# A second place for the next expert's transposed rows in an attention and mixture-of-experts kernel

## The chip, the core and the metric

The kernel runs on one core of one Trainium2 chip. The metric is the device time of one execution in microseconds; the median of three executions of the kernel before is 756.62 us (755.61 to 757.49). The core's engines are called PE (TensorE), ACT (ScalarE), DVE (VectorE), POOL (GpSimd) and SP (SyncE, which here issues most of the DMAs). Each of them works through its own instructions in order, and waits on semaphores for the others.

## What is computed

The reference first does causal attention with a decay, for 8 batches, 8 heads, 576 positions and 64 columns per head, and reshapes the result to 4608 rows of 512 columns. Then it does a mixture of eight experts, each row in one expert:

```
logits = x @ w_gate;  e_idx = argmax(logits, axis=1)
gate_w = softmax(logits) at e_idx;  eom = sigmoid(x @ w_output_gate)
for e in range(8):
    mask = e_idx == e
    h  = maximum(x[mask] @ w1[e], 0)        # 512 -> 1024
    ye = h @ w2[e]                          # 1024 -> 512
    out[mask] = gate_w[mask] * eom[mask, e] * ye
```

The change touches only the second half, from about 345 us on.

## The kernel before

All values are carried as two 16-bit parts (a high part in f16 and the rest), so a product is made of three matmuls. The attention stage also computes for each of its rows the expert, the row's rank in it and its weight; it writes the rows to a DRAM buffer `xbuf`. The instructions of each engine stand in the order in which the program text makes them (`manual_schedule`), so every line of the text sets a place in each queue it touches.

**The experts.** Expert 0 is done first, with rows of early batches and plain products (`up`, `down`). Expert 1 follows. The other six are ordered by how many rows they have: a small chain on DVE (lines 1396 to 1425) sums up the counts, sorts them, and writes `rank` (which expert comes n-th) and `ids` (its rows and weights). The n-th expert is given a fixed capacity, `CAPS` = 640, 608, 592, 576, 560, 512 rows; expert 1 has 640. Rows beyond these capacities go to lists of overflow (`overflow_slots`, lines 1016 to 1052), which the loop at the end of the program works off; it has no work here, but its count `ncum` must be loaded into a register of every engine (line 1485).

**Up products (`up_seven`).** The product with `w1` is done blockwise with seven block products in place of eight: weights and rows are first added and subtracted in blocks. For the weights this is `weights_pair` (four of them per expert): DVE makes sums in PSUM, POOL (or DVE, with `pool=False`) makes the difference `xr` in SBUF, ACT makes the high parts, DVE and POOL the low ones. For the rows it is `rows_whole` (POOL, four additions of high and low part into f32 tiles `x`) and `rows_sums` (called for k = 0 and 1: DVE subtracts, ACT casts, DVE makes the low part, four times). Each `up_seven` runs four rounds `p` of seven products (each product six matmuls); ACT copies three partial results of a round to `keep` (`kept`, line 1289), where DVE takes them up in its additions (lines 1313, 1317, 1323). The last product of a round is put into the next round; that of the last round is made within the first down tile (`finish_up`). Twice per round `between(p, half)` does side work, numbered `fc` = 0 to 7: ACT and POOL split one block of `w2`, SP fetches another, POOL gathers rows of the next expert, SP fetches its `w1`.

**Rows of the next expert.** `gather_rows(x, t)` is an indirect DMA from POOL of 128 rows into `xg[:, t]`; `gather_turn(x, t)` is a DMA transpose from SP's queue of those rows into `xT`. `rows_x` makes the tile `xT` in a pool with one buffer. In the kernel before it is always the pool `m2`:

```
if nx:
    x1 = rows_x(m2, nx["ids"])
```

so the next expert's transposes write where the current expert's products read.

**Down products.** For each tile of 128 rows `down_sum` makes 24 matmuls of 512 columns into one of two PSUM banks `y`; ACT scales it into `ys` (line 1102) and POOL writes it out by indirect DMA (line 1106). The rest of a capacity beyond whole tiles is done by `down_narrow` in parts of 64 and 32 rows, which DVE evicts (lines 1131, 1133); the last tile of the last expert is done in two halves of columns (`down_halves`). Beside tile `t` of the down products stands a piece of work for the next expert: before the change a `weights_pair` beside t = 0, 1, 3 and 4, `rows_whole` at t = 1 ahead of its pair, and both `rows_sums` beside t = 2.

PSUM tiles for sums come from one ring of three banks (`hp1`), which block products, `weights_pair` and `rows_sums` share.

Of the kernel before, what the change touches and what calls it, by code (L numbers as in the profile page):

```python
# [9 lines left out]
F32 = mybir.dt.float32  # L10
# [10 lines left out]
P = 128  # L21
# [3 lines left out]
E = 8  # L25
# [16 lines left out]
CAP = 640  # L42
CT = CAP // P
FIXED = 2
# [5 lines left out]
ET = 3  # L50
# [27 lines left out]
def _attn_moe(ctx, tc, qk, vm, f, wg, w1, w2, out):  # L78
# [937 lines left out]
    def overflow_slots():  # L1016

        with tc.tile_pool(name="ov", bufs=1) as ov:
            g = [ov.tile([P, E, G], F32, name=f"ov{j}") for j in range(3)]
            start, eid = [ov.tile([P, E, G], BF16, name=f"g{j}") for j in range(2)]  # L1020
            me, caps = [ov.tile([P, n], F32, name=f"c{n}") for n in (1, E)]
            for t, pattern, base in ((start, [[0, E], [P, G]], 0), (eid, [[1, E], [0, G]], 0)):
                nc.gpsimd.iota(t, pattern=pattern, base=base, channel_multiplier=0,
                               allow_small_or_imprecise_dtypes=True)
            nc.gpsimd.iota(me, pattern=[[0, 1]], base=1, channel_multiplier=1, allow_small_or_imprecise_dtypes=True)
            for r, cap in enumerate(CAPS + [CAP] * FIXED):
                nc.gpsimd.memset(caps[:, r:r + 1], float(cap))
            mine = ov.tile([P, E, E], F32, name="mine")
            own, over = [ov.tile([P, E], F32, name=n) for n in ("own", "over")]
            nc.vector.tensor_tensor(mine, key.unsqueeze(2).broadcast_to([P, E, E]),  # L1030
                                    top.unsqueeze(1).broadcast_to([P, E, E]), op=ALU.is_equal)
            nc.vector.tensor_tensor(mine, mine, caps.unsqueeze(1).broadcast_to([P, E, E]), op=ALU.mult)
            nc.vector.tensor_reduce(own, mine, axis=AX.X, op=ALU.add)
            nc.vector.tensor_tensor(over, cnt, own, op=ALU.subtract)
            fl = lambda t: t.rearrange("p e g -> p (e g)")
            valid, cum, base = g
            nc.vector.tensor_tensor(valid, over.unsqueeze(2).broadcast_to([P, E, G]), start, op=ALU.is_gt)
            nc.vector.tensor_tensor_scan(fl(cum), fl(valid), fl(valid), 0.0, op0=ALU.add, op1=ALU.max)
            nc.vector.scalar_tensor_tensor(fl(base), fl(eid), float(NT), fl(start), op0=ALU.mult, op1=ALU.add)
            nc.vector.tensor_tensor(base, base, own.unsqueeze(2).broadcast_to([P, E, G]), op=ALU.add)  # L1040

            nc.vector.scalar_tensor_tensor(fl(valid), fl(cum), me, fl(valid), op0=ALU.is_equal, op1=ALU.mult)
            res = ov.tile([P, 2], F32, name="res")
            for j, src in ((1, base), (0, eid)):
                nc.vector.tensor_tensor(base, src, valid, op=ALU.mult)
                nc.vector.tensor_reduce(res[:, j:j + 1], fl(base), axis=AX.X, op=ALU.add)
            resi = ov.tile([P, 2], I32, name="resi")
            nc.vector.tensor_copy(resi, res)
            nc.sync.dma_start(slots, resi)
            ncum = cp.tile([1, 1], I32, name="ncum")  # L1050
            nc.vector.tensor_copy(ncum, fl(cum)[0:1, E * G - 1:E * G])
        return ncum
# [208 lines left out]
    def up_seven(ws, x, sums, cap, h, between):  # L1261
# [21 lines left out]
            nc.vector.scalar_tensor_tensor(hl[:, fc, sl], m, 0.0, hh[:, fc, sl], op0=ALU.max, op1=ALU.subtract)  # L1283
            yield

        keep = ar.tile([P, 2048], F32, name="x")[:, 0:6 * CAP // 2].rearrange("p (j n) -> p j n", j=6)

        def kept(j, m):
            nc.scalar.copy(out=keep[:, j, 0:n], in_=m)  # L1289
# [8 lines left out]
        for p in range(HF):  # L1298
            w = ws[p]
            y = staged(n, "hp0")  # L1300
            product(y, w, A11, rows_of_half(0, 0), True)
            p1 = kept(p % 2, y)
            z = staged(n)
            product(z, w, S1, rows_sum(T1), True)
            p5 = kept(2 + p % 2, z)
            if open_:
                last_product(*open_)
            between(p, 0)
            product(y, w, S2, rows_sum(T2), False)
            u2 = kept(4 + p % 2, y)  # L1310
            v = staged(n)
            product(v, w, A12, rows_of_half(1, 0), True)
            nc.vector.tensor_tensor(v, v, p1, op=ALU.add)  # L1313
            product(z, w, S4, rows_of_half(1, 1), False)
            c11, c12 = split(v, p, 0), split(z, p, 1)
            next(c11)
            nc.vector.tensor_tensor(z, z, u2, op=ALU.add)
            next(c11)
            next(c12)
            between(p, 1)  # L1320
            product(y, w, S3, rows_sum(T3), False)
            u = staged(n, "y")
            nc.vector.tensor_tensor(u, y, p5, op=ALU.add)
            next(c12)
            for _ in split(u, p + HF, 1):
                pass
            open_ = p, w, y
# [5 lines left out]
    with tc.manual_schedule(engines=ENGINES):  # L1333
# [3 lines left out]
        feats_out(NQ - 1)  # L1337
        W1r = {fc: fetch_w1(m2, w1[1], fc, 8) for fc in PAIRS}
        AHEAD = 4
        slot = m1.tile([P, CT], F32, name="slot")  # L1340
        nc.gpsimd.iota(slot, pattern=[[P, CT]], base=0, channel_multiplier=1, allow_small_or_imprecise_dtypes=True)
        beyond = m1.tile([P, len(CAPS), CT], F32, name="beyond")
# [38 lines left out]
            gather_turn(x1, t)  # L1381
        first_splits(1, 2)
        down_out(x, down_sum(W2, h, 0), 0)
        first_splits(2, 3)
        down_out(x, down_sum(W2, h, 1), 1)
        first_splits(3, HF)
        down_out(x, down_sum(W2, h, 2), 2)
        sums = rows_whole(x1, CAP)
        up(W1, x, [(EARLY, CAP)], h)
        for k in range(2):  # L1390
            rows_sums(sums, CAP, k)
        down(W2, xl, h, ET, CT)
        W1, W2, x = W1n, [], x1

        cnt_ps = pr.tile([P, 512], F32, name="ms", bufs=1)
        nc.tensor.matmul(cnt_ps[:, 0:E], ones16, runs, start=True, stop=True)
        cnt = cp.tile([P, E], F32, name="cnt")
        nc.vector.tensor_copy(cnt, cnt_ps[:, 0:E])
        nc.vector.tensor_tensor(cnt[:, 0:1], cnt[:, 0:1], late, op=ALU.add)
        tie, key, top = [m1.tile([P, E], F32, name=n) for n in ("tie", "key", "top")]  # L1400
        rank = m1.tile([P, E], I32, name="rank")
        nc.gpsimd.iota(tie, pattern=[[1, E]], base=0, channel_multiplier=0, allow_small_or_imprecise_dtypes=True)
        nc.gpsimd.memset(tie[:, 0:FIXED], -1e6)
        nc.vector.scalar_tensor_tensor(key, cnt, float(E), tie, op0=ALU.mult, op1=ALU.add)
        nc.vector.max(top, key)
        nc.vector.tensor_copy(rank, top)
# [8 lines left out]
        for j in range(2):  # L1415
            each = m1.tile([P, R, CT, E], F32, name="each")
            shape = [P, R, CT, E]
            nc.vector.tensor_tensor(each, acc[:, j].rearrange("p e t -> p t e").unsqueeze(1).broadcast_to(shape),
                                    mine.unsqueeze(2).broadcast_to(shape), op=ALU.mult)
            if j:  # L1420
                nc.vector.tensor_reduce(ids[:, :, :, 1].bitcast(F32), each, axis=AX.X, op=ALU.add)
            else:
                own = m1.tile([P, R, CT], F32, name="own")
                nc.vector.tensor_reduce(own, each, axis=AX.X, op=ALU.add)
                nc.vector.tensor_tensor(ids[:, :, :, 0], own, beyond, op=ALU.add)

        def expert(r):

# [7 lines left out]
        for n in range(len(CAPS) + 1):  # L1436
# [2 lines left out]
            nx = expert(n) if n < len(CAPS) else None  # L1439
            nt = -(-nx["cap"] // P) if nx else 0  # L1440
            if nx:
                x1 = rows_x(m2, nx["ids"])

            def between(p, half):
                fc = 2 * p + half
                W2.append(split_w2(W2r[fc], nc.gpsimd))
                if fc + AHEAD < NF:
                    W2r.append(fetch_w2(e["w2"], fc + AHEAD))
                if nx:
                    if 2 <= fc < 2 + nt:  # L1450
                        gather_rows(x1, fc - 2)
                    if fc >= NF - AHEAD:
                        g = PAIRS[fc - NF + AHEAD]
                        W1r[g] = fetch_w1(m2, nx["w1"], g, 8)

            finish_up = up_seven(W1, x, sums, cap, h, between)
            W1n, W2n = [], []
            for t in range(nt):
                gather_turn(x1, t)
            for t in range(tiles):  # L1460
                if nx is None and t == tiles - 1:
                    down_halves(W2, x, h, t)
# [3 lines left out]
                if nx:  # L1466
                    for g in PAIRS[2 * t + AHEAD:2 * t + AHEAD + 2]:
                        W1r[g] = fetch_w1(m2, nx["w1"], g, 8)
                    if t == 1:
                        sums_n = rows_whole(x1, nx["cap"])  # L1470
                    if t == 2:
                        for k in range(2):
                            rows_sums(sums_n, nx["cap"], k)
                    else:
                        W1n.append(weights_pair(W1r, len(W1n)))
                    if t == 3:
                        W2r = [fetch_w2(nx["w2"], fc) for fc in range(AHEAD)]
# [1 line left out]
                    down_narrow(W2, x, h, t, rest)  # L1479
                else:  # L1480
                    down_out(x, y, t)
                if n == 0 and t == 3:
                    ncum = overflow_slots()
                if n == 2 and t == 0:
                    nsl = nc.values_load(ncum, min_val=0, max_val=(NT - min(CAPS)) // P + E)
            if nx:
                e, x, W1, W2, sums = nx, x1, W1n, W2n, sums_n
# [73 lines left out]
```

## Time and profile before

| | us |
|---|---|
| median of three executions | 756.62 |
| the profiled execution, its whole time | 753.45 |
| its span, first to last instruction | 751.7 |
| PE matmuls busy | 693.3 (92% of the span) |
| POOL busy | 551.9 (73%) |
| DVE busy | 519.7 (69%) |
| ACT busy | 415.4 (55%) |

A line of the timeline has the start and the length in us, the engine, the line of the program, the operation, the tile written and the tiles read, the shapes, how many instructions are merged, and in brackets how long the engine was idle before it and whose work ended that wait. Matmuls overlap in the array: those of 512 columns show 0.38 us each but start every 0.215 us.

### The profile page before, as it was taken

To read this page: it belongs to the slowest core of one execution; us is meant where nothing else is said; L and a number is where in the kernel's file an instruction comes from. 1 tells how busy PE (TensorE), PEld (TensorE's weight loads), DVE (VectorE), ACT (ScalarE), POOL (GpSimd) and SP (SyncE) were. 2 spreads that over 40 slices of the span, in tenths; PEclk is the share of its full clock that TensorE was granted. 3 is DMA by queue.
4 is the path that set the end of the run, shared out by engine and by line. 5 is a ranking of instruction groups with operands and counts; after the bars stand their busy time and mean duration, and the time that the engine had idled before them with its cause. 6 is when DMAs were issued, how large, how long until landed. Compare 5 with 4: busy or idle time off the path is not lost. (4 is left out here: it accounts for less than half of the span.)

```text
span 751.7 us, 22240 instructions
## 1 busy us (share of the span) xinstructions
PE 693.3 (92%) x8823; PEld 460.1 (61%) x8842; DVE 519.7 (69%) x1175; ACT 415.4 (55%) x990; POOL 551.9 (73%) x618
## 2 busy tenths in 40 slices
PE   4999999999999999989989949989979899799896
PEld 2577777777777777765746426547447366374564
DVE  7576798999989978778575574555585576656640
ACT  4456666667666756654345436456456465464641
POOL 9879799999899989824436745767757687687632
PEclk9999999999999999999999978999999999999999
DMA  4436577667766663394815604824917638348101
GB/s 153 157 120 181 161 186 191 182 168 167 190 174 170 149 172 75 98 228 129 188 63 155 195 28 157 210 90 154 238 48 187 199 101 204 132 154 224 60 15 39
DMA packets 119452, 110.72 MB, mean 147 GB/s; under 512 B 82669, under 2 KB 92077, under 8 KB 119344
## 3 DMA queue, kind: packets, MB, share of 16 engines
q1 hardware_dynamic: 108566, 71.50, 37.8%
q10 hardware_dynamic: 4618, 18.88, 7.7%
q0 software_dynamic: 6160, 18.88, 7.6%
q8 instruction: 70, 1.15, 0.6%
q14 instruction: 38, 0.31, 0.2%
HBM read 72.47 MB, written 19.49 MB: 122 GB/s over the span
## 5 line engine op out<-in xcount | busy, mean ns | idle before, releaser
L434 POOL TENSOR_TENSOR plo<-p 128x512 f16<-128x512 f32 x182 | 194.4, 1087 | 21.5 <-PE mx L305 11.6
L1276 PE MATMUL hp<-xT,sh 128*128 128x320 f16 (+5 forms) x784 | 152.8, 295 | 21.8 <-ACT x L1289 17.0
L432 ACT ACTIVATE p<-sc 128x512 f32<-128x512 f32 x192 | 111.6, 595 | 60.6 <-PE sc L305 58.5
L336 DVE TENSOR_REDUCE nR<-mx 128x2 f32<-128x1024 f32 (+4 forms) x154 | 121.3, 805 | 34.4 <-PE mx L305 32.0
L1276 PE MATMUL hp<-xT,sl 128*128 128x320 f16 (+5 forms) x392 | 115.3, 294 | 0.0
L305 PE MATMUL sc<-qk 64*128 64x64 f32 (+5 forms) x644 | 114.0, 432 | 0.0
L1090 PE MATMUL y<-w2h,hh 128*128 128x512 f16 x272 | 103.7, 381 | 5.2 <-ACT ys L1102 5.2
L1276 PEld LDWEIGHTS <-sh 128*128 128x128 f16 x784 | 77.6, 100 | 50.1 <-issue 24.9
L1092 PE MATMUL y<-w2h,hl 128*128 128x512 f16 x272 | 103.7, 381 | 1.2 <-issue 0.2
L1091 PE MATMUL y<-w2l,hh 128*128 128x512 bf16 x253 | 96.4, 381 | 0.0
L1010 POOL TENSOR_TENSOR w2l<-w2r,w2h 128x512 bf16<-128x512 f32 x56 | 64.7, 1157 | 37.9 <-ACT w2h L1009 31.0
L305 PEld LDWEIGHTS <-pick 64*128 64x128 bf16 (+1 forms) x1152 | 55.0, 97 | 55.1 <-issue 41.7
L1281 ACT ACTIVATE hh<-hp 128x320 f16<-128x320 f32 (+5 forms) x84 | 34.9, 417 | 60.1 <-DVE hp L1313 31.0
L505 PE MATMUL av<-Vs,p 128*128 128x65 f16 x640 | 65.9, 193 | 1.3 <-ACT xr L552 1.3
L506 PE MATMUL av<-Vs,p 128*128 128x64 bf16 x640 | 65.7, 195 | 0.0
L507 PE MATMUL av<-Vs,plo 128*128 128x65 f16 x640 | 65.4, 192 | 0.0
L1106 POOL DMA_INDIRECT out_dram<-ys,idsr x28 | 28.0, 999 | 49.1 <-ACT ys L1102 35.4
L305 PE MATMUL mx<-qk 64*128 64x512 bf16 (+3 forms) x372 | 54.9, 308 | 8.5 <-DMA qk<-in_qk_dram 5.9
L505 PEld LDWEIGHTS <-p 128*128 128x128 bf16 x640 | 59.1, 97 | 5.5 <-issue 5.3
L1283 DVE SCALAR_TENSOR_TENSOR hl<-hp,hh 128x320 f16<-128x320 f32 (+5 forms) x84 | 38.6, 459 | 33.2 <-ACT hh L1281 27.3
L506 PEld LDWEIGHTS <-p 128*128 128x128 bf16 x640 | 59.4, 97 | 1.4 <-issue 1.4
L507 PEld LDWEIGHTS <-plo 128*128 128x128 f16 x640 | 59.4, 99 | 0.0
(262 smaller groups left out, 1826.2 us busy)
## 6 DMA issues: line engine op xcount, KB each, us to landing
qk<-in_qk_dram ACTq DMA_DIRECT2D x31, 576.0 KB
w1r<-in_w_dram SPq DMA_DIRECT2D x64, 256.0 KB
w2r<-in_w_dram SPq DMA_DIRECT2D x64, 256.0 KB
v<-in_vm_dram SPq DMA_DIRECT2D x15, 576.0 KB
xbuf<-x SPq DMA_DIRECT2D x16, 512.0 KB
Eq<-mts SPq DMA_DIRECT2D x64, 0.1 KB
xbuf<-x SPq DMA_DIRECT2D x16, 64.0 KB
xT<-x SPq DMA_TRANSPOSE x62
```

What stands on the lines that cost most here:

```text
L305: nc.tensor.matmul(dst(i), w(i), x(i), start=start, stop=stop)
L336: nc.vector.tensor_reduce(o, x, axis=AX.X, op=ALU.max, negate=True)
L432: nc.scalar.activation(out=f32, in_=src, func=AF.Exp, scale=0.125)
L434: eng.tensor_tensor(lo, f32, upper(f32), op=ALU.subtract)
L505: nc.tensor.matmul(dst, ph, vv[:, 0:W], start=kc == 0, stop=False)
L506: nc.tensor.matmul(dst[:, 0:D], ph, vv[:, W:].bitcast(BF16), start=False, stop=False)
L507: nc.tensor.matmul(dst, pl, vv[:, 0:W], start=False, stop=kc == qc)
L1010: eng.tensor_tensor(l, raw, h, op=ALU.subtract)
L1090: nc.tensor.matmul(y, hh[:, fc, sl], wh, start=j == 0, stop=False)
L1091: nc.tensor.matmul(y, hh[:, fc, sl], wl, start=False, stop=False)
L1092: nc.tensor.matmul(y, hl[:, fc, sl], wh, start=False, stop=j == NF - 1)
L1276: nc.tensor.matmul(m, w[part][:, j, k], b(q, k), start=first and k == i == 0, stop=k == 1 and i == 2, skip_group_check=True)
```

## The change

Six edits, all in the expert stage:

- The next expert's `xT` is taken from `m2` for odd n and from the pool `ar` for even n. `gather_rows` moves from `fc` 2 to 6 to `fc` 0 to 4, and `gather_turn` from behind `up_seven` into `between`, two steps behind its gather.
- `rows_whole` moves from t = 1 to ahead of the first down tile; `rows_sums` is made for k = 0 beside t = 1, ahead of the pair that is there, and for k = 1 beside t = 2.
- `keep` has a tile of its own with three slots, in place of six slots in a tile of `x`.
- The chain of counts, ranks and `ids` moves from behind expert 0 into it, behind the first down tile; its constants `tie` are made earlier.
- The fourth weight pair of expert 1 (`first_splits(3, HF)`) moves from behind down tile 1 of expert 0 to behind the row sums.
- `overflow_slots` moves from t = 3 of expert 1 to t = 0 of the last expert, with three of its tiles in an old tile `x16`, and the load of its count moves from the third expert of the loop to the last one's last tile but one.

```diff
@@ overflow_slots
-            g = [ov.tile([P, E, G], F32, name=f"ov{j}") for j in range(3)]
+            g = ar.tile([P, 1280], F32, name="x16", bufs=2)[:, 0:3 * E * G]
+            g = [g[:, j * E * G:(j + 1) * E * G].rearrange("p (e g) -> p e g", g=G) for j in range(3)]
@@ up_seven
-        keep = ar.tile([P, 2048], F32, name="x")[:, 0:6 * CAP // 2].rearrange("p (j n) -> p j n", j=6)
+        keep = m1.tile([P, 3, CAP // 2], F32, name="keep")
...
-            p1 = kept(p % 2, y)
+            p1 = kept(0, y)
...
-            p5 = kept(2 + p % 2, z)
+            p5 = kept(1, z)
...
-            u2 = kept(4 + p % 2, y)
+            u2 = kept(2, y)
@@ expert 0
+        tie, key, top = [m1.tile([P, E], F32, name=n) for n in ("tie", "key", "top")]
+        nc.gpsimd.iota(tie, pattern=[[1, E]], base=0, channel_multiplier=0, allow_small_or_imprecise_dtypes=True)
+        nc.gpsimd.memset(tie[:, 0:FIXED], -1e6)
...
         down_out(x, down_sum(W2, h, 0), 0)
-        first_splits(2, 3)
-        down_out(x, down_sum(W2, h, 1), 1)
-        first_splits(3, HF)
-        down_out(x, down_sum(W2, h, 2), 2)
-        sums = rows_whole(x1, CAP)
-        up(W1, x, [(EARLY, CAP)], h)
-        for k in range(2):
-            rows_sums(sums, CAP, k)
-        down(W2, xl, h, ET, CT)
-        W1, W2, x = W1n, [], x1
-
         cnt_ps = pr.tile([P, 512], F32, name="ms", bufs=1)
         nc.tensor.matmul(cnt_ps[:, 0:E], ones16, runs, start=True, stop=True)
...
                 nc.vector.tensor_tensor(ids[:, :, :, 0], own, beyond, op=ALU.add)
+        first_splits(2, 3)
+        down_out(x, down_sum(W2, h, 1), 1)
+        down_out(x, down_sum(W2, h, 2), 2)
+        sums = rows_whole(x1, CAP)
+        up(W1, x, [(EARLY, CAP)], h)
+        for k in range(2):
+            rows_sums(sums, CAP, k)
+        first_splits(3, HF)
+        down(W2, xl, h, ET, CT)
+        W1, W2, x = W1n, [], x1
@@ the loop over experts
-                x1 = rows_x(m2, nx["ids"])
+                x1 = rows_x(m2 if n % 2 else ar, nx["ids"])
...
                 if nx:
+                    if fc < nt:
+                        gather_rows(x1, fc)
                     if 2 <= fc < 2 + nt:
-                        gather_rows(x1, fc - 2)
+                        gather_turn(x1, fc - 2)
...
-            for t in range(nt):
-                gather_turn(x1, t)
+            if nx:
+                sums_n = rows_whole(x1, nx["cap"])
...
-                    if t == 1:
-                        sums_n = rows_whole(x1, nx["cap"])
-                    if t == 2:
-                        for k in range(2):
-                            rows_sums(sums_n, nx["cap"], k)
-                    else:
+                    if t in (1, 2):
+                        rows_sums(sums_n, nx["cap"], t - 1)
+                    if t != 2:
                         W1n.append(weights_pair(W1r, len(W1n)))
...
-                if n == 0 and t == 3:
+                if nx is None and t == 0:
                     ncum = overflow_slots()
-                if n == 2 and t == 0:
+                if nx is None and t == tiles - 2:
                     nsl = nc.values_load(ncum, min_val=0, max_val=(NT - min(CAPS)) // P + E)
```

## Rows read from the trace of the kernel before

**Rows 1.** The page, 40 slices of the span: granted clock of PE in tenths.

```profile
PEclk9999999999999999999999978999999999999999
```

**Rows 2.** Waits of PE, 380 to 752 us: us in total, times, longest us.

```profile
PE hp L1276 <- ACT x L1289: 17.0, 6, 8.4
PE y L1123 <- ACT ys L1102: 7.7, 5, 2.5
PE y L1090 <- ACT ys L1102: 5.2, 2, 2.6
PE hp L1276 <- DVE y L1323: 4.6, 3, 2.9
```

**Rows 3.** Timeline of PE, 380 to 460 us: start us, us, idle in brackets.

```profile
393.24 0.43 PE L1276 MATMUL hp<-xT,sh 128*128 128x320 f16 x2 [2.86 <-DVE y L1323]
...
434.72 0.38 PE L1090 MATMUL y<-w2h,hh 128*128 128x512 f16 x1 [2.60 <-ACT ys L1102]
...
451.82 0.69 PE L1276 MATMUL hp<-xT,sh 128*128 128x320 f16 x2 [8.44 <-ACT x L1289]
```

**Rows 4.** Busy time by engine in one stretch; behind POOL: PEclk, DMA share, GB/s.

```profile
430.00:440.00 10.00, 7.18 (x26) 2.97 (x26) 6.77 (x15) 5.67 (x13) 4.88 (x6) 0.83 0.07 26
```

**Rows 5.** Timeline of SP's queue, 440 to 500 us.

```profile
473.57 7.40 SPq L822 DMA_TRANSPOSE xT<-xg  x5
```

**Rows 6.** Timeline of POOL, 451 to 506 us.

```profile
467.77 1.02 POOL L816 DMA_INDIRECT xg<-xbuf,idsr  x1 [0.15 <-issue]
...
475.22 1.15 POOL L1010 TENSOR_TENSOR w2l<-w2r,w2h 128x512 bf16<-128x512 f32 x1 [0.72 <-ACT w2h L1009]
...
483.10 5.44 POOL L1234 TENSOR_TENSOR x<-xT 128x608 f32<-128x608 f16 x4 [0.57 <-DMA xT<-xg]
```

**Rows 7.** Timeline of ACT, 451 to 512 us.

```profile
489.26 0.41 ACT L1202 CAST sh<-xr 128x256 f16<-128x256 f32 x1 [5.81 <-POOL xr L1208]
...
490.15 0.40 ACT L1247 CAST xT<-hp 128x304 f16<-128x304 f32 x1
...
497.43 0.41 ACT L1247 CAST xT<-hp 128x304 f16<-128x304 f32 x1 [0.48 <-DVE hp L1246]
```

**Rows 8.** Waits of SP's queue, 452 to 506 us.

```profile
SPq L822 <- DMA xg<-xbuf,idsr: 4.7, 1, 4.7
```

**Rows 9.** Timeline of ACT, 722 to 752 us: one down tile after another.

```profile
734.69 0.69 ACT L1102 ACTIVATE ys<-y,idsr 128x512 f32<-128x512 f32 x1 [4.49 <-PE y L1092]
```

**Rows 10.** Timeline of DVE, 451 to 512 us: start of one weight pair, of the next.

```profile
498.45 0.42 DVE L1207 TENSOR_TENSOR hp<-w1r 128x256 f32<-128x256 f32 x1
...
501.40 0.49 DVE L1207 TENSOR_TENSOR hp<-w1r 128x256 f32<-128x256 f32 x1
```

**Rows 11.** Timeline of DVE, 547 to 570 us.

```profile
552.71 1.43 DVE L1207 TENSOR_TENSOR hp<-w1r 128x256 f32<-128x256 f32 x1
...
558.99 2.32 DVE L1133 SCALAR_TENSOR_TENSOR ys<-y,idsr,ys 32x512 f32<-32x512 f32 x3
```

**Rows 12.** Timeline of DVE, 437 to 449 us: the overflow lists.

```profile
437.67 0.90 DVE L1030 TENSOR_TENSOR mine<-key,top 128x64 f32<-128x64 f32 x1
441.43 0.74 DVE L1032 TENSOR_TENSOR mine<-mine,c 128x64 f32<-128x64 f32 x1 [2.86 <-POOL c L1027]
...
448.26 0.14 DVE L1051 CAST ncum<-ov 1x1 int32<-1x1 f32 x1
```

**Rows 13.** Instructions of line 1485, duration min/median/max in ns.

```profile
L1485 PEldq TENSOR_LOAD <-ncum x1: 793/793/793, 529.6 to 529.6; - x1
```

**Rows 14.** Timeline of DVE, 330 to 402 us.

```profile
358.14 0.42 DVE L1207 TENSOR_TENSOR hp<-w1r 128x256 f32<-128x256 f32 x1
...
360.55 1.28 DVE L1205 TENSOR_TENSOR sl<-hp,sh 128x512 bf16<-128x512 f32 x2
...
384.44 0.16 DVE L1398 COPY cnt<-ms 128x8 f32<-128x8 f32 x1
...
387.34 1.11 DVE L1404 SCALAR_TENSOR_TENSOR key<-cnt,tie 128x8 f32<-128x8 f32 x1 [2.48 <-POOL tie L1402]
```

More of the change, by code (lines that the diff above doesn't have):

```diff
@@ L1399, in _attn_moe @@
         nc.vector.tensor_tensor(cnt[:, 0:1], cnt[:, 0:1], late, op=ALU.add)
-        tie, key, top = [m1.tile([P, E], F32, name=n) for n in ("tie", "key", "top")]
         rank = m1.tile([P, E], I32, name="rank")
-        nc.gpsimd.iota(tie, pattern=[[1, E]], base=0, channel_multiplier=0, allow_small_or_imprecise_dtypes=True)
-        nc.gpsimd.memset(tie[:, 0:FIXED], -1e6)
         nc.vector.scalar_tensor_tensor(key, cnt, float(E), tie, op0=ALU.mult, op1=ALU.add)
```

## The prediction

> **What bounds the kernel now.** I read the page first, then TensorE's (PE's) waits in the expert stage, then the stretches around its gaps. The page shows PE busy in nearly every slice, at full clock but for a few [rows 1]. So what an edit is worth is what it takes from PE's gaps. From 380 us on these are 35.0 us, in four kinds [rows 2]: 17.0 behind ScalarE's (ACT's) copies at the head of a seven-product stage, 12.9 (7.7 and 5.2) behind ACT's `ys`, which empties a down-product bank, 4.6 behind VectorE (DVE). The timeline gives their places; the largest of B and C stand in [rows 3]. By transition from one expert to the next, in us of idle: B, into the first seven-product expert 3.7; C 11.3 (8.44 of it the overflow stall, 2.6 `ys`); D 3.5; E 5.3; F 2.9; G 4.9; H 3.4.
>
> Behind the longer gaps PE's clock falls: mean 0.83 of 2.4 GHz over a slice of 10 us [rows 4], that is 3.4 us at 1.2 GHz, in which 1.7 us of work is lost. I find five such dips (one each in B, F and H, two in C) and take 1.5 us each.
>
> Why the gaps are there: the row transposes wait on SyncE's (SP's) queue until the current expert's products have read the one `xT`. In D they start at 473.57, as those products end (U = 474.2) [rows 5]. GpSimd (POOL) is through with its split at 476.4, but `rows_whole` begins at 483.1 only [rows 6]. The next weight pair's `xr` stands behind it, so ACT waits 5.81 us for that; then 7.7 us of row sums follow without a `ys` between, and PE waits for the third one [rows 7].
>
> **The change part by part.**
>
> *Second place for `xT`, gathers two halves earlier, transposes within the products.* Counts stay: five gathers, five transposes, the same weight fetches. What matters is when the last transpose lands. The fifth gather takes the place of the one at 467.77 now [rows 6]; it lands at most 4.7 us later (SP's wait for a gather [rows 8]), 472.5; one transpose is a fifth of 7.4 us [rows 5], 474.0; landing adds 2.0 (the five are issued by 480.97, POOL starts at about 483.0), so 476.0. POOL is free at 476.4. Slack: 0.4 us. Behind a transpose that waits for its gather, SP holds back one weight fetch by about 4 us; that fetch is made four halves of 2.9 us ahead, which hides it. The next `w1` blocks now stand behind transposes three to five on SP; the two of the first pair are issued by about 471 and needed at 477.5. Bounds: at worst the transposes land when they do now, 6.7 us later; at best POOL's own work sets the start.
>
> *The sums in two output tiles.* Worked out for D from U = 474.2; a down tile is 5.18 us of PE [rows 9], the first 6.0 as it holds the last product. PE could end tiles at 480.2, 485.4, 490.6, 495.8. POOL: `rows_whole` 476.4 to 481.8, `xr` to 482.5. ACT: last cast 0.4, `ys0` 0.7: 483.7; the third tile needs that at 485.4, so the 2.6 us stall goes. One half of the sums takes 4.0 (from 490.15 a half is 3.9, plus the last subtract) [rows 7]: 487.7. The pair's DVE work is 3.0 [rows 10]: 490.7; `ys1` 491.1. Tile four could start at 490.6, so 0.5 stays. Second half to 495.1, `ys2` ends by then; tile five can start at 496.3. Pairs three and four follow to about 501.7 on ACT, `ys4` 502.4, first kept copy 502.8; PE begins the next expert at 501.5 and needs that copy two products (1.6) later, 503.1. So what is late next is `ys1`, by half a microsecond.
>
> For C this leaves 0.8 (larger matrices), for D 0.5. E and F have a narrow last tile, whose six DVE evictions (4.6 us, the last three of them 2.3) run before the next expert's additions [rows 11]: 0.4 in the down part and 1.4 to 1.5 at the second pair, 1.8 and 1.9. G and H have a narrow tile of 2.6 us only, so PE is at the next expert before ACT is: 1.7 and 1.3. Together 8.0, against 31.3 now (C to H): 23.3 gained. Idles that short have no dip behind them in this trace, so four of the five dips go: 6.0. Below, if all stalls of this kind stay near 2 us, the gain of C to H is some 10 less; above, nothing stays: 8 more.
>
> A row that speaks against it: beside POOL's work one DVE sum of two SBUF operands took 1.43 us [rows 11], where the same one takes 0.42 in a quiet place [rows 10]; that 1.0 falls on pair 0's DVE work, which has 2 us of slack before `ys0`, so I add nothing. The Trainium skill (SBUF — State Buffer, Who interferes with whom) says that a DVE instruction with two SBUF inputs and a GpSimd one that reads SBUF exclude each other, the later one blocked wholly. The trace agrees in size. By the rule alone one collision of 1.0 us on the way to `ys1` in each of six transitions would take 6 off the sum, to 735.
>
> *`keep` with three slots in its own tile.* A copy now waits for the additions of the pair before; those end before it is due. Nothing; 0.3 per expert at worst.
>
> *Overflow lists at the last expert.* Now: DVE from 437.67 to 448.40, 2.9 of it waiting for POOL's constants [rows 12]. Pair four is queued behind it, ACT behind that, PE behind ACT: 8.44. All goes from here. There, after tile 0 of the last expert, DVE has nothing to do. POOL makes the constants behind the `put` of tile 0 (730.5 in the present trace) and is through 2.2 us later, 732.6; DVE's 7.0 us from there give the count at 739.6. PE has two tiles to do until 739.7. But the load of the count is now just there: PE's load takes 0.79 [rows 13], so PE stands still 0.8 before the last tile. The load on the other four engines, and the small list that SP writes, lie beside PE's last 5.3 us. From 0 (the chain ends early) to 3 (it ends two us late). Taking the load out of expert 2 saves nothing: PE's queue hid it.
>
> *Ranks earlier.* Of DVE's 6.9 us from 384.44 on, 2.5 are a wait for POOL's `tie` [rows 14], which is now made ahead. The other 4.4 move to 354.5, between pairs 1 and 2: pair 2 ends at 362.5, before DVE's first split at 363.6, so hidden there, with the one small matmul and the `tie` constants.
>
> *Pair 3 behind the row sums.* DVE 3.7 us [rows 14] at 384.5, where the ranks were. ACT must do the casts of that pair's sums before two `ys` and the first kept copy: 384.5 + 1.5 (four sums) + 1.1 (two casts) + 1.3 (two `ys`, as long as in the same stretch now) = 388.4, copy to 388.8. PE stops after its second product and resumes at 388.8, some 3.4 us later than now; six products of 0.82 on is 393.7, where now it resumes at 393.24 after the wait behind the ranks. Idle 4.5 instead of 3.7, the dip as before: 0.8 lost. From 3 lost to 3 gained (no dip).
>
> **Sum.** 23.3 + 6.0 − 0.8 − 0.8 = 27.7. Profiled execution 753.45 (span 751.7 and 1.75 around it), so 725.7; the median of the runs shown is 3.2 above the profiled one: 728.9, say 729.
>
> **Rivals.**
> - *Half filled*: ACT's and DVE's chains in tiles one and two are longer than I put them (port collisions, casts), so about 2 us per transition stay. For: only 0.5 us of room in tile four. Against: the chain is put together from measured pieces. 10 less: 739.
> - *Only the overflow stall goes*: C's 8.4 and one dip, the rest as now: 756.6 − 9.9 + 1.6 = 748. For: the DMAs are close to full while transposes run. Against: the down stage no longer has them.
> - *Slower*: `rows_whole` now stands on POOL before all four pairs. If the transposes still land 6.7 us after POOL is free, `xr`, the cast, `ys0` and everything behind come 6.7 later; with slack 1.8 once, then none, each of six transitions pays 6.7 more. 6 × 6.7 = 40 against 27.7: 12 slower, 769. It decides from a landing 27.7 / 6 = 4.6 us after POOL is free. For: SP issues in order, and now waits in it. Against: room of several halves.
> - *Better*: nothing left at the narrow tiles and in B: 720.
> - *It does not do what it says* (the second place is not free, so the transposes wait as now) is the slower rival's case.
>
> **How the numbers follow.** Forecast 729 (722 to 736) 0.62; half filled 739 0.19; overflow only 748 0.06; slower 769 0.05; better 720 0.08. The range 721 to 742 holds the first two and most of the last. A difference under 0.3% (2.3 us) can't be told from none in this measurement. Faster 0.94, same 0.01, slower 0.05: only the slower rival ends above, and a sliver between.
>
> **What would show it.** PE's wait behind ACT's copies falls from 17.0 to under 6, and no single gap of 8; transposes start within the products and POOL's `rows_whole` begins within 3 us of their end; the rows with ACT waiting 5.8 for `xr` go; B's gap sits before the third product, not the ninth; PE has a gap under 1.5 before the last tile, with the overflow work beside tiles one and two. I am wrong if `rows_whole` still waits for DMA by more than 2 us, or if `ys1` holds PE by 2 us.

## The result, and the profile after

The changed kernel takes 735.16 us (median of four executions, 731.35 to 736.71); the kernel before, run beside it, 757.06 us (755.61 to 759.55). The ratio is 0.970, with a 95% interval of 0.9652 to 0.9748: 2.9% faster. The forecast was 729 with a range of 721 to 742. The sign and most of the mechanism held; about a fifth of the gain is missing (21.9 of 27.7 us).

The page of the changed kernel shows the granted clock of PE in 40 slices. The two slices that stood at 7 and 8 [rows 1] have become one of 8.

```profile
PEclk9999999999999999999998999999999999999999
```

PE's waits in the expert stage of the changed kernel (380 to 735 us; us in total, times, longest): 19.1 us in place of 35.0 [rows 2]. The single stall of 8.4 is gone, the waits behind `ys` fell from 12.9 to 7.6, and those behind `y`, DVE's, from 4.6 to 2.4.

```profile
PE hp L1277 <- ACT keep L1290: 7.9, 7, 3.1
PE y L1091 <- ACT ys L1103: 7.6, 7, 1.7
PE hp L1277 <- DVE y L1324: 2.4, 2, 1.2
PE hp L1277 <- DVE xT L1251: 1.2, 1, 1.2
```

PE's timeline has their places (start, length, idle in brackets). The first two lines are B, the third C, which had 2.60 and 8.44 [rows 3]; the next three are E, then come F and G.

```profile
388.75 0.43 PE L1277 MATMUL hp<-xT,sh 128*128 128x320 f16 x2 [1.23 <-DVE xT L1251]
...
392.81 0.69 PE L1277 MATMUL hp<-xT,sh 128*128 128x320 f16 x2 [3.08 <-ACT keep L1290]
...
434.00 0.38 PE L1091 MATMUL y<-w2h,hh 128*128 128x512 f16 x1 [1.46 <-ACT ys L1103]
...
533.51 0.38 PE L1091 MATMUL y<-w2h,hh 128*128 128x512 f16 x1 [1.73 <-ACT ys L1103]
...
545.41 0.41 PE L1277 MATMUL hp<-xT,sh 128*128 128x296 f16 x2 [0.83 <-ACT keep L1290]
...
551.24 0.41 PE L1277 MATMUL hp<-xT,sh 128*128 128x296 f16 x2 [1.14 <-DVE y L1324]
...
584.12 0.38 PE L1091 MATMUL y<-w2h,hh 128*128 128x512 f16 x1 [1.70 <-ACT ys L1103]
...
645.53 0.40 PE L1277 MATMUL hp<-xT,sh 128*128 128x280 f16 x2 [1.85 <-ACT keep L1290]
```

The stages, each from the first down product of one expert to the end of the next expert's up rounds (B: the up rounds of expert 1 alone; tail: the last down products), by the two profiled executions, in us. Two neighbours overlap by up to 0.2, since the matmuls do. "Idle" is the sum of PE's waits in the stage.

| | before | after | gained | forecast | idle before | idle after | idle forecast |
|---|---|---|---|---|---|---|---|
| B | 28.1 | 29.7 | −1.6 | −0.8 | 3.7 | 4.3 | 4.5 |
| C | 63.9 | 51.0 | 13.0 | 13.5 | 11.3 | 1.7 | 0.8 |
| D | 51.7 | 48.7 | 3.0 | 3.0 | 3.5 | 0.5 | 0.5 |
| E | 52.0 | 50.4 | 1.6 | 3.5 | 5.3 | 3.7 | 1.8 |
| F | 50.5 | 50.0 | 0.5 | 2.5 | 2.9 | 3.6 | 1.9 |
| G | 48.9 | 48.2 | 0.7 | 3.2 | 4.9 | 3.9 | 1.7 |
| H | 47.1 | 43.5 | 3.6 | 3.6 | 3.4 | 1.2 | 1.3 |
| tail | 21.6 | 21.6 | 0 | −0.8 | 0 | 0 | 0.8 |

The sum of "gained" is 20.8. The profiled execution of the changed kernel lies 1.55 above its median; it begins expert 1 at 386.54, where four kernels below (experiments 2, 3, 5 and 7), whose code is the same up to there, begin at 383.1 to 383.5. So its attention part ran some 3 us long, and the stages are compared, not the spans.

D and H do as forecast, C nearly; E, F and G keep most of the idle time they had. POOL's timeline of the changed kernel has the reason. The `rows_whole` of D, E, F and G stand at 469.19, 519.29, 570.13 and 620.27 (in the kernel before D's was at 483.10 [rows 6]): D's waits 0.22, the others 1.81, 2.37 and 2.69.

```profile
460.46 1.02 POOL L816 DMA_INDIRECT xg<-xbuf,idsr  x1 [0.16 <-PE hp L1277]
...
467.82 1.15 POOL L1010 TENSOR_TENSOR w2l<-w2r,w2h 128x512 bf16<-128x512 f32 x1 [1.89 <-ACT w2h L1009]
469.19 5.39 POOL L1235 TENSOR_TENSOR x<-xT 128x608 f32<-128x608 f16 x4 [0.22 <-issue]
...
509.31 1.02 POOL L816 DMA_INDIRECT xg<-xbuf,idsr  x1 [0.16 <-PE hp L1277]
...
519.29 5.37 POOL L1235 TENSOR_TENSOR x<-xT 128x592 f32<-128x592 f16 x4 [1.81 <-DVE hl L1284]
...
549.63 0.94 POOL L1107 DMA_INDIRECT out_dram<-ys,idsr  x1 [2.66 <-DVE ys L1134]
...
551.92 1.07 POOL L816 DMA_INDIRECT xg<-xbuf,idsr  x1 [0.16 <-issue]
...
561.48 1.02 POOL L816 DMA_INDIRECT xg<-xbuf,idsr  x1 [0.16 <-issue]
...
566.61 1.16 POOL L1010 TENSOR_TENSOR w2l<-w2r,w2h 128x512 bf16<-128x512 f32 x1 [1.69 <-ACT w2h L1009]
570.13 5.19 POOL L1235 TENSOR_TENSOR x<-xT 128x576 f32<-128x576 f16 x4 [2.37 <-issue]
...
599.86 0.92 POOL L1107 DMA_INDIRECT out_dram<-ys,idsr  x1 [2.65 <-DVE ys L1134]
...
620.27 5.05 POOL L1235 TENSOR_TENSOR x<-xT 128x560 f32<-128x560 f16 x4 [2.69 <-DMA xT<-xg]
```

Only G's wait is labelled with the DMA. E's and F's labels name another releaser; I read them as the same wait. In experiments 3, 4 and 5 E's wait carries the DMA's label, in experiment 9 F's does, and in experiments 5 to 9 moving gathers and fetches shortens these waits. The rows show two different delays. In F and G the write-out (`put`) of the narrow tile waits 2.66 and 2.65 for DVE's evictions, and the five gathers stand behind it, 2.4 us apart: from the last gather to `rows_whole` it is 8.7 in F as in D, but that gather starts 6.3 ahead of the end of POOL's last split (567.77) and not 8.5 (468.97). In E there is no narrow tile ahead, and the gather is not late (8.2 ahead of the last split's end at 517.48); from it to `rows_whole` it is 10.0.

The windows of the changed kernel (busy time by engine; behind POOL the clock, the DMA share, GB/s): the first line is B's dip, the second E's transposes, during which the share of the 16 DMA engines is 1.11.

```profile
390.00:400.00 10.00, 7.18 (x33) 4.28 (x33) 4.57 (x10) 5.51 (x12) 4.78 (x5) 0.66 0.28 93
...
510.00:520.00 10.00, 9.95 (x67) 6.39 (x66) 5.76 (x14) 6.04 (x15) 4.49 (x5) 1.00 1.11 193
```

DVE's timeline of the changed kernel: the second pair sum of C and the first of D, both beside POOL's work, the second of F, and the overflow lists at their new place, where POOL has only their constants and a write-out to do.

```profile
429.85 1.39 DVE L1208 TENSOR_TENSOR hp<-w1r 128x256 f32<-128x256 f32 x1
...
470.64 1.47 DVE L1208 TENSOR_TENSOR hp<-w1r 128x256 f32<-128x256 f32 x1
...
580.93 0.42 DVE L1208 TENSOR_TENSOR hp<-w1r 128x256 f32<-128x256 f32 x1
...
710.24 0.21 DVE L1031 TENSOR_TENSOR mine<-key,top 128x64 f32<-128x64 f32 x1
715.85 0.23 DVE L1033 TENSOR_TENSOR mine<-mine,c 128x64 f32<-128x64 f32 x1 [5.39 <-POOL c L1028]
...
721.15 0.14 DVE L1052 CAST ncum<-x 1x1 int32<-1x1 f32 x1
```

### The profile page after: what moved, and what is told of

The parts are those of the page before. It is cut to its first block, busy times and chain, and to the rows that moved or that the text cites. A ratio compares the mean times of both kernels' runs of the same rounds, so it can differ in the third digit from the quotient of the medians.

```text
span 735.0 us, 22266 instructions
## 1 busy us (share of the span) xinstructions
PE 690.8 (94%) x8823; PEld 457.4 (62%) x8842; DVE 514.5 (70%) x1175; ACT 415.4 (57%) x990; POOL 554.6 (75%) x618
## 5 line engine op out<-in xcount | busy, mean ns | idle before, releaser
L1277 PE MATMUL hp<-xT,sh 128*128 128x320 f16 (+5 forms) x784 | 150.8, 292 | 11.5 <-ACT keep L1290 7.9
L305 PE MATMUL mx<-Ek,Eq 63*128 63x512 f16 (+3 forms) x372 | 55.0, 299 | 2.9 <-DMA Ek<-d 2.9
```

The costliest lines, as they stand in the source:

```text
L305: nc.tensor.matmul(dst(i), w(i), x(i), start=start, stop=stop)
L1277: nc.tensor.matmul(m, w[part][:, j, k], b(q, k), start=first and k == i == 0, stop=k == 1 and i == 2, skip_group_check=True)
```

## The experiments

Medians are of four executions (six in experiment 2 and in 10 to 12). The kernel before, beside them, had 757.98 (1 to 4), 756.46 (5 to 7), 754.48 (8 and 9) and 756.27 (10 to 12).

**1. The overflow part alone**, in the kernel before:

```diff
-                if n == 0 and t == 3:
+                if nx is None and t == 0:
                     ncum = overflow_slots()
-                if n == 2 and t == 0:
+                if nx is None and t == tiles - 2:
```

> The kernel before with one part of the change: the overflow lists and the load of their count at the last expert. Theory 'the 8.44 us stall is the lists on VectorE': the stall and the dip behind it go, 9.9 us, and 0 to 0.8 comes at the last tile: 747 where before is 757, ratio 0.987; the other gaps stay. Rival 'something behind the lists (the write-out, the fourth pair) fills the gap': under 3 us, ratio over 0.996.

747.98 us, ratio 0.9878 (0.9836 to 0.9919). PE's waits of this kernel:

```profile
PE y L1123 <- ACT ys L1102: 7.7, 5, 2.2
PE y L1090 <- ACT ys L1102: 6.6, 3, 3.0
PE hp L1276 <- ACT x L1289: 5.3, 3, 3.0
PE hp L1276 <- ACT xT L1247: 4.6, 1, 4.6
```

The stall of 8.4 is gone and nothing takes its place in C; the up rounds of the expert behind it take 22.2, as in the changed kernel (22.6). This one edit is worth some 10 us, nearly half of the whole gain. The rest of the change brings 13 more.

**2. The transposes behind the products again** (one place for `xT`), all else as changed:

```diff
-                x1 = rows_x(m2 if n % 2 else ar, nx["ids"])
+                x1 = rows_x(m2, nx["ids"])
...
-                    if 2 <= fc < 2 + nt:
-                        gather_turn(x1, fc - 2)
...
+            for t in range(nt):
+                gather_turn(x1, t)
             if nx:
                 sums_n = rows_whole(x1, nx["cap"])
```

> The changed kernel, but the next expert's transposed rows go into the one old place, so the transposes stand behind the products again; all else as changed, rows_whole ahead of the first down tile. Theory 'the landing of the last transpose is the price of the new order': rows_whole starts some 6 us later, and each of six transitions pays 4 to 6.7 us: 735 + 24 to 40 = 759 to 775, not faster than before. Rival 'the place matters little, the new order of the sums is what counts': at most 6 us, under 741.

764.3 us (757.51 to 767.5), ratio 1.0073 (1.0027 to 1.0119): 0.7% slower than the kernel before. POOL's timeline of this kernel, the first two of six such rows, and PE's first wait:

```profile
425.16 5.69 POOL L1235 TENSOR_TENSOR x<-xT 128x640 f32<-128x640 f16 x4 [6.06 <-DMA xT<-xg]
...
483.30 5.43 POOL L1235 TENSOR_TENSOR x<-xT 128x608 f32<-128x608 f16 x4 [7.59 <-DMA xT<-xg]
```

```profile
PE y L1091 <- ACT ys L1103: 27.4, 8, 5.6
```

Here the forecast's slower rival is real: `rows_whole` ahead of the first tile, with transposes that land 4.7 to 7.6 late, hands the wait through `xr`, the cast and `ys` to PE. Without the second place the changed kernel is 29 us slower. It is also 16 us slower than the kernel of experiment 1, which keeps the old order of the down stage (the two differ in `keep`, the ranks and the fourth pair as well). So the new order makes sense only with the second place.

**3. Both sums beside one tile again**, all else as changed:

```diff
-                    if t in (1, 2):
-                        rows_sums(sums_n, nx["cap"], t - 1)
-                    if t != 2:
+                    if t == 2:
+                        for k in range(2):
+                            rows_sums(sums_n, nx["cap"], k)
+                    else:
                         W1n.append(weights_pair(W1r, len(W1n)))
```

> The changed kernel, but both row sums beside the third output tile, as before. Theory A 'early transposes are what opens the chain, the split of the sums adds nothing': with transposes early the second ys is free at once, the third comes about when the fifth tile wants it: within 2 us of 735. Theory B 'the sums in two tiles are half of the gain': the 2.6 us stall before the fifth tile is back in each transition, 735 + 6 x 2 = 747.

743.64 us, ratio 0.982 (0.9777 to 0.9862): 8.5 more than the changed kernel, between the two values expected. PE's waits of this kernel, and the clock (the number behind POOL) in two of its stretches:

```profile
PE hp L1277 <- ACT keep L1290: 10.2, 6, 2.9
PE y L1124 <- ACT ys L1103: 6.0, 4, 2.0
PE hp L1277 <- DVE xT L1251: 4.6, 1, 4.6
```

```profile
540.00:550.00 10.00, 9.94 (x81) 5.96 (x78) 8.46 (x14) 5.67 (x14) 8.28 (x10) 0.83 0.15 54
...
650.00:660.00 10.00, 10.00 (x75) 7.66 (x73) 5.07 (x13) 5.59 (x15) 8.55 (x10) 0.86 0.44 112
```

PE's idle in C to H is 18.6, 3.9 more than in the changed kernel, but these stages together are 8.8 us longer. The rest is clock: behind waits of 2.02, 2.89 and 2.06 us it falls again, as it did in the kernel before (0.83, 0.86 and 0.86 over 10 us), while in the changed kernel it stays full from C to H. B has another 2.5 of idle, ahead of anything the edit touches, but PE also began expert 1 some 3 us earlier here. So the split over two tiles is worth some 8.5 us, less than the second place.

**4. The fourth pair of expert 1 at its old place**, all else as changed:

```diff
         down_out(x, down_sum(W2, h, 1), 1)
+        first_splits(3, HF)
         down_out(x, down_sum(W2, h, 2), 2)
...
-        first_splits(3, HF)
         down(W2, xl, h, ET, CT)
```

> The changed kernel, but the fourth weight pair of expert 1 where it was, beside expert 0's second down tile (the ranks stay early). Theory 'the 4.3 us of idle and the clock dip at the head of expert 1 come from that pair's casts ahead of the first kept copy': both go, 4 to 6 us less than 735, 730; the early pair costs up to 1 us in expert 0's products. Rival 'the wait only takes another name, since VectorE is behind by its row sums anyway': within 1.5 us of 735.

729.11 us, ratio 0.9621 (0.9573 to 0.9668). PE's timeline of this kernel around B: 1.17 lost in expert 0's products, 0.76 idle in B (4.31 before the edit), no dip, and B takes 23.3 in place of 29.7.

```profile
363.18 0.38 PE L1065 MATMUL hp<-xT,w1h 128*128 128x256 f16 x2 [1.17 <-DVE hl L1075]
...
382.59 0.45 PE L1277 MATMUL hp<-xT,sh 128*128 128x320 f16 x2 [0.21 <-ACT xT L1248]
...
384.13 0.43 PE L1277 MATMUL hp<-xT,sh 128*128 128x320 f16 x2 [0.55 <-ACT keep L1290]
```

POOL's timeline of this kernel, `rows_whole` of D:

```profile
461.55 5.44 POOL L1235 TENSOR_TENSOR x<-xT 128x608 f32<-128x608 f16 x4 [4.02 <-DVE hp L1211]
```

Moving that pair behind the row sums was a loss of about 6 us inside the change. With the ranks early as well, the old place costs the 1.2 us in expert 0's products. One stage speaks of chance: D's code is that of the changed kernel, but here `rows_whole` waited 4.02 in D in place of 0.22, and D took 52.3 in place of 48.7.

**5. The first two gathers of the next expert ahead of the last tile's write-out**, so that they don't stand behind the `put` that waits for DVE (`ahead = 2 if n else 0`):

```diff
-                    if fc < nt:
-                        gather_rows(x1, fc)
+                    if fc < nt - ahead:
+                        gather_rows(x1, fc + ahead)
...
+                if last:
+                    for k in range(2):
+                        gather_rows((ids[:, n + 1], None), k)
                 if y is None:
```

> The changed kernel, but the first two gathers of an expert stand at the end of the expert before, ahead of the last tile's write-out on GpSimd; the other three take the first three halves. Theory P 'GpSimd's queue makes the last transpose late: with a narrow tile its write-out waits 2.7 us for VectorE and five gathers then run in a row with the splits': the fifth gather is 4 to 5 us earlier, GpSimd's wait of 1.8, 2.4 and 2.7 us ahead of rows_whole in E, F and G goes under 0.5, PE's waits behind ys there (1.7 each, and 0.2 to 0.4) fall by 4 to 6 us together: 730. Theory D 'the DMA engines are full while transposes run, so the last one lands when it does': the waits stay over 1.5, within 1 us of 735.

732.32 us, ratio 0.968 (0.9644 to 0.9716). `rows_whole` waits 2.30, 0 and 0.90 in E, F and G (1.81, 2.37 and 2.69 before the edit), PE's waits behind `ys` fall from 7.6 to 5.0. The two with the narrow tile gain, E doesn't. The time alone can't be told from that of the changed kernel, since the intervals overlap.

**6. Experiments 4 and 5 together.**

> The gathers ahead as in the run beside it and the fourth weight pair of expert 1 at its old place. If the two gains add: 729 less 4 to 6, 724; by theory D 728 to 729.

723.07 us, ratio 0.9551 (0.9495 to 0.9607): the time comes out as if the gains added. But `rows_whole` waits 1.97, 1.71 and 2.43 in this execution, hardly less than in the changed kernel. SP's queue of this kernel shows F: behind the third transpose and a `w1` fetch it stands 4.7 us for the fourth gather, which POOL had issued at 542.93.

```profile
543.20 3.63 SPq L822 DMA_TRANSPOSE xT<-xg  x2
547.07 0.39 SPq L778 DMA_DIRECT2D w1r<-in_w_dram  x1
...
552.27 1.23 SPq L822 DMA_TRANSPOSE xT<-xg  x1
```

POOL's timeline has the fifth gather and `rows_whole`:

```profile
545.31 1.02 POOL L816 DMA_INDIRECT xg<-xbuf,idsr  x1 [0.16 <-PE hp L1277]
...
557.89 5.31 POOL L1235 TENSOR_TENSOR x<-xT 128x576 f32<-128x576 f16 x4 [1.71 <-issue]
```

From the one to the other it is 12.6 here, against 8.7 in the changed kernel: the gather leaves earlier and takes longer. The DMA share is 1.16 from 545 to 555. So POOL's order isn't the whole cause; the next three experiments try the load of the DMA engines.

**7. The four `w1` fetches of the last halves behind the last transpose**, all else as changed:

```diff
-                    if fc >= NF - AHEAD:
-                        g = PAIRS[fc - NF + AHEAD]
-                        W1r[g] = fetch_w1(m2, nx["w1"], g, 8)
...
             if nx:
+                for g in PAIRS[0:AHEAD]:
+                    W1r[g] = fetch_w1(m2, nx["w1"], g, 8)
                 sums_n = rows_whole(x1, nx["cap"])
```

> The changed kernel, but the four fetches of the next w1 that stand between the last three transposes on SyncE's queue stand behind them: 1 MB less for the DMA engines while the transposes run. Theory D: GpSimd's waits ahead of rows_whole in E, F and G fall under 0.7 us. Theory P: they stay within 0.6 us of 1.8, 2.4 and 2.7. In both the first weight pair waits 1 to 3 us for its blocks, so the time is 735 to 745 and the wait is the reading.

734.93 us, ratio 0.9711 (0.9664 to 0.9757): no different from the changed kernel. `rows_whole` waits 0, 1.84, 1.88 and 0.71 in E to H. E's wait is gone, and PE's idle in C to H is 12.0 (14.7 in the changed kernel), although DVE and ACT now wait 4.7 and 4.0 for the weights that come later. In this execution B stood idle 7.5, ahead of anything the edit touches, so the two equal medians don't tell what the edit is worth.

**8. As 6, and the four `w1` fetches made one down stage earlier** (at t = 3 of the expert before, so that during the transposes there are only `w2` fetches):

```diff
-                    if fc >= NF - AHEAD:
+                    if fc >= NF - AHEAD and n == 0:
...
                     if t == 3:
+                        if n + 1 < len(CAPS):
+                            nn = expert(n + 1)
+                            for g in PAIRS[0:AHEAD]:
+                                W1r[g] = fetch_w1(m2, nn["w1"], g, 8)
```

> The run with the gathers ahead and the fourth pair at its old place (723), and besides the four fetches of w1 that stood among the transposes are made one down stage earlier, beside the fourth tile, when the DMA engines are idle: 1 MB less for them while the transposes run, and nothing later for the pairs. Theory D (the DMA engines set when the last transpose lands): GpSimd's waits of 2.0, 1.7 and 2.4 us ahead of rows_whole in E, F and G go under 0.7, the waits behind ys there from 1.7 to under 0.7: 723 less 3 to 5, 719. Theory P (GpSimd's queue does): already spent, 722 to 724.

722.56 us, ratio 0.9579 (0.9519 to 0.964). POOL's timeline of this kernel, F and G: no wait but 0.82 in G.

```profile
556.06 5.15 POOL L1235 TENSOR_TENSOR x<-xT 128x576 f32<-128x576 f16 x4
...
603.89 5.03 POOL L1235 TENSOR_TENSOR x<-xT 128x560 f32<-128x560 f16 x4 [0.82 <-DMA xT<-xg]
```

PE's waits behind `ys` are 2.0, and its idle in C to H 8.6 (13.9 in experiment 6), though the median is not told apart from that of 6.

**9. As 4, and the early `w1` fetches, with the gathers as changed.**

> The same early fetches of w1 in the kernel with the fourth pair at its old place (729), gathers as in the changed kernel. Theory D: the waits ahead of rows_whole in E, F and G fall from 1.9, 2.9 and 2.6 by 1 to 2 us each, 726. Theory P: they stay, 729. If only both edits together take the waits away, this one stays within 1 us of 729 and the one beside it reaches 719.

724.28 us, ratio 0.9598 (0.9539 to 0.9657). `rows_whole` waits 0, 1.76 and 1.84 in E, F and G, PE behind `ys` 4.4 (9.7 in experiment 4). E's wait is gone in all three kernels with the fetches moved (7, 8, 9) and in neither with the gathers alone (5, 6). By its time this kernel can't be told from that of 8.

**10 to 12. The kernels of 4, 6 and 8 once more, on one chip, in six executions each**, since their intervals overlap above.

> The kernel of experiment 4 (the fourth pair of expert 1 at its old place) on the same chip as the two that follow, so that the three can be compared. In its first profile PE stood idle 17.1 us in transitions C to H. Expected: ratio to the kernel before 0.962, 727 to 730 us. It is the base of the two others: call its median T.

> The kernel of experiment 6 (as above, and the first two gathers ahead of the last write-out). Theory 'POOL's order': the late gathers are the cause, so this alone brings nearly all, T less 7 to 8, and the earlier w1 fetches add under 1. Theory 'both': idle in C to H was 13.9 in its first profile, 3.2 under T's, so T less 3 to 4. If the landing of the transposes costs no time in the end, T less 0 to 1.

> The kernel of experiment 8 (as above, and the four w1 fetches a down stage earlier). Idle in C to H was 8.6 in its first profile, 8.5 under T's. Theory 'both': T less 8 to 9, and 4 to 5 under the kernel ahead of it. Theory 'POOL's order': within 1 of the kernel ahead of it. If the earlier fetches cost elsewhere what they bring, no better than T.

729.07, 725.50 and 721.49 us; ratios 0.9634 (0.9593 to 0.9674), 0.9583 (0.9531 to 0.9636) and 0.9534 (0.9492 to 0.9576). PE's waits behind `ys` in the three, one line from each:

```profile
PE y L1091 <- ACT ys L1103: 8.4, 7, 1.7
```

```profile
PE y L1091 <- ACT ys L1103: 4.9, 3, 1.7
```

```profile
PE y L1091 <- ACT ys L1103: 2.3, 2, 1.6
```

Idle in C to H is 15.0, 11.5 and 8.8. By the medians the gathers bring 3.6, the earlier fetches another 4.0, as the theory of two causes had it (3 to 4, then 4 to 5). Only the ends, 7.6 apart, have intervals that don't overlap; neither step by itself is clear of the noise. Of E, F and G, `rows_whole` waits 0.49, 3.30 and 2.70 in the first, 2.12, 0 and 2.12 in the second; in the third 0.91 in G alone. Single waits differ by up to 1.7 between two executions of the same code (F in 6 and in 11), so a verdict hangs on the sums and not on one of them. The sums of the three waits, over all kernels that have them, part cleanly: 6.5 to 8.0 with neither edit (the changed kernel and experiments 3, 4 and 10), 3.2 to 6.1 with the gathers alone (5, 6, 11), 3.6 and 3.7 with the fetches alone (9, 7), 0.8 and 0.9 with both (8, 12). Each edit shortens the waits, and only both take them away. The kernel of 8 and 12 beats both kernels: 721.49 is 4.7% under the kernel before, and 1.9% under the median of the changed one.

## Why the prediction was right, and where it was short

- **The overflow stall: right.** C's forecast was 13.5, measured 13.0, and the edit alone gives 748, which is what the forecast's rival "only the overflow stall goes" had worked out for it.
- **The second place and the order of the down stage: right in D and H**, to 0.1 us in the stage. In D that is in part luck: the same code waited 4.02 in experiment 4 and 1.25 in experiment 10, where the forecast had 0.4 to spare. Experiment 2 shows the condition the slower rival named: with landings 4.7 to 7.6 after POOL is free, the kernel is slower than before (764; 769 was worked out).
- **The clock: right.** C to H gained 22.4, of which 16.6 is idle time (31.3 less 14.7). The other 5.8 is where the forecast put its 6.0 for four dips: 3.5 in C, 1.2 in F, 1.4 in H, less 0.2 in G. In the changed kernel every 10 us of C to H (410 to 710) are at a granted clock of 1.00.
- **The step that failed: the 5.4 us of idle left in E, F and G** (1.8, 1.9, 1.7), which measured 11.3. The forecast worked out one transition, D, with 0.4 of slack between POOL's last split and the landing, and used it for all. For the narrow tiles it added what DVE's six evictions do to PE's next rounds (1.4 to 1.5 at the second pair; measured 1.14 in E and 1.23 in F), but not what they do to POOL: the `put` waits 2.66 for them, five gathers stand behind it, and in F and G the slack becomes a lack of 2.4 and 2.7 (in D it measured a lack of 0.2). It had counted what stands behind each wait on SP, and not on POOL. And it took the time from the last gather to `rows_whole` as one number, 8.2 (467.77 to 476.0); D, F and G have 8.6 to 8.7, but E has 10.0, and where gathers leave earlier into full DMA engines it was up to 12.6. With both causes eased (experiments 8 and 12) the idle left in C to H is 8.6 and 8.8, close to the 8.0 forecast. By stages E, F and G fall 6.4 short of the forecast, B and C 1.3 more, and the tail gives 0.8 back.
- **C's idle, 1.7 for 0.8.** Its second pair's sum runs beside a split of POOL's that begins at 429.79 and takes 1.39 (0.42 in F), and PE's wait of 1.46 for `ys1` is right behind it; experiment 8 has the same 1.39 and 1.45, with no wait for a landing. By the Trainium skill (SBUF — State Buffer, Who interferes with whom) a DVE instruction with two SBUF inputs excludes a GpSimd one that reads SBUF; in C the trace agrees. The forecast's alternative by that rule, one such collision on the way to `ys1` in each transition and 735 in all, gives the very time that was measured, but not for its reason: in F the sum took 0.42 and PE waited 1.70 for `ys` all the same, and in D it took 1.47 on the first pair and PE waited 0.4.
- **B: the place right, the size short.** The gap of 3.08 is before the third product, as forecast (another 1.23 before the second). B's idle is 4.3 against 4.5, but the clock falls further behind it (0.66 in place of 0.83 over that slice), so the stage lost 1.6 where 0.8 was put. Even that is the shortest seen: in the four kernels with the same code up to there B took 30.2 to 33.8, with PE at expert 1 some 3 us earlier. Experiment 4 shows that the move as such costs 6: the forecast compared with B of before, and didn't ask what B would be with the ranks gone and the pair left in its place.
- **The tail: 0 for −0.8.** DVE's chain took 5.4 (715.85 to 721.29), not 7.0, and PE's load of the count is no longer just late.
- **By the prediction's own signs:** no gap of 8, `ys1` under 2 us, the place of B's gap: as stated. PE behind ACT's copies is 7.9 where "under 6" was written (3.1 of it B). And the sign against it, `rows_whole` waiting for a DMA by more than 2 us, showed in F and G (2.37, 2.69). The median of 735 lies within the forecast's 722 to 736, but nearer to the rival "half filled" (739), which has the wrong cause: not ACT's and DVE's chains, but a landing.

What stays open: why the transposes of expert 1 land at different times in different executions (B's idle, with the pair at its new place, was 4.3, 5.9, 6.9, 7.5 and 8.0 in five kernels with the same code up to there), and why E's landing takes longer than F's: the DMA share is 1.11 in E and 1.12 in F, so the share doesn't tell them apart, and in experiment 10 E's wait was 0.49 with neither edit. Neither was tried. Nor do the runs part two readings of the fetches: moving them takes load from the DMA engines, and it also takes two fetches of some 0.4 us each from between the last transposes on SP's own queue.

## What to carry to other kernels

A stage that repeats with other sizes is to be worked out for each size: a forecast slack of 0.4 us behind a full tile was a lack of 2.4 behind a narrow one, because one write-out at the head of a queue waited for another engine and five gathers stood behind it. When an edit takes work away from a place, ask anew about everything else that was moved to make room there: one of the six moves here cost about 6 us, net of the 1.2 that its old place costs. A second buffer is worth its price only if what fills it arrives in time, so follow the last transfer back to its issue, through the order of the queue and through what else is in flight; easing one of the two gave about half, by the medians.

## What the runs showed of the hardware that was not expected

- Small DVE instructions can pay for POOL's work as well as large ones. The instruction that makes `mine` in the overflow lists took 0.90 and 0.74 beside POOL's work [rows 12], and 0.21 and 0.23 in the tail, where POOL was idle beside them; the whole chain took 7.0 there and 5.4 here.
- A gather that leaves POOL four microseconds earlier may land hardly earlier: with the DMA engines at a share of 1.16 it took 12.6 us from the fifth gather to the sums that wait for its transpose (experiment 6, F), and 8.7 where it left later. In experiments 5 and 11, with the gathers at the same place, F's sums did not wait; there it is 11.0, and POOL's own work sets its end.
